# In the expert stage, weight splits and last products of the word conversion move from GpSimd to VectorE, sign and magnitude to ScalarE

## The chip, the cores and the metric

The kernel runs on one core of a Trainium2 chip. The metric is the device time of one execution in microseconds (us); the median of several executions is compared. TensorE (PE) multiplies, with weight loads (PEld) beside it; VectorE (DVE), ScalarE (ACT) and GpSimd (POOL) work element by element; SyncE (SP) issues most DMAs. Each engine works through its own instructions in order.

## The reference

Three parts follow each other: an attention whose scores below a threshold are dropped, a mixture of eight experts of which each token takes one, and a dense layer with the activation h - tanh(h). Weights of the dense layer (`w_in`, `w_out`) are float64.

```python
scores = scale * q @ k.T; thresh = max(scores) - tau
attn = exp(where(scores >= thresh, scores, -1e9) - max); attn /= sum(attn)
x = attn @ v                                   # 2304 tokens x 512

expert_idx = argmax(x @ w_gate)                # one of E = 8 experts for each token
h = maximum(xe @ w1[e], 0.0)                   # w1[e]: 512 x 1024
out[mask] = gate_w * (h @ w2[e])               # w2[e]: 1024 x 512

h = x @ w_in                                   # 512 x 2048, float64 weights
return ((h - tanh(h)) @ w_out).astype(float32) # 2048 x 512
```

## The kernel before

The three parts run after each other: attention to about 350 us, routing to about 370, the experts to about 650, the dense layer to the end. In the experts and the dense layer each matrix product is made three times on TensorE, from high and low parts of the operands: high is the value rounded to a short mantissa (a ScalarE copy to fp32r), low is the rest (a subtraction).

**Groups.** The expert stage is a row of 72 groups of work, numbered g: nine passes (the experts ranked by token count, the second one in two passes) of 256, 256, 288, 416, 384, 336, 320, 288 and 272 tokens, and eight groups for each pass. In group g, `h_exp` makes 12 matmuls into one of two PSUM buffers; `relu` (L1075, L1076) takes the high part by ScalarE and the low one by VectorE into `hbuf`; then come the jobs that the planner has put into group g; then `y_exp` makes the 12 matmuls of the second product for group g - 2. So `h` of group g + 2 waits until VectorE has read `h` of group g.

**The jobs** are entered by `plan` through `at(group, function)`, and in one group they are issued in the order in which `plan` enters them: token gathers (GpSimd, `gather_exp`, an indirect DMA, ten groups ahead of their pass), transposes of the gathered tokens (TensorE, one PSUM buffer "t"), their evacuation into high and low parts (L1027 by ScalarE, L1031 by VectorE), weight loads (`wload`, SP, four or five groups ahead) and weight splits (`wsplit`), loads of the dense layer, the late part of the routing (from group 8 on, a job in every second group), and last the word conversion.

**Weight splits.** `wload` brings 128 x 1024 words of w1 or w2 into one of four `raw` buffers. `wsplit` copies the high part by ScalarE (L1008) and subtracts it (L1010): by VectorE for w1, by GpSimd for w2 (all j = 1 with r < E). For the dense layer (r == E) the table `"eng"` says which engine subtracts.

**The word conversion.** `conv` turns the float64 words of the dense layer's weights into float32, 128 x 512 values at a time, in 32 conversions that start at the groups of the table `"conv"` (0 to 57). Its four steps stand in the groups start + 0, 3, 4 and 5 (table `"cv"`): `load` (SP, into one of three `cv` buffers); `bits` (three VectorE instructions: shift of the high word, L1155, joining with the low word, L1157, a mask for very negative values, L1159); `sign` (magnitude by ScalarE, L1163, a sign of -1, 0 or 1 by VectorE, L1164, their product by GpSimd, L1166); `store` (SP, to DRAM). The buffer `cm` has two halves that conversions use in turn, so that conversion n + 2 writes its half only after conversion n is stored.

Of the kernel before, what the change touches and what calls it, by code (L numbers as in the profile page):

```python
# [11 lines left out]
F32 = mybir.dt.float32  # L12
F32R = mybir.dt.float32r
F16 = mybir.dt.float16
BF16 = mybir.dt.bfloat16
I32 = mybir.dt.int32
U32 = mybir.dt.uint32
AF = mybir.ActivationFunctionType
ALU = mybir.AluOpType
# [409 lines left out]
E, F1, F2 = 8, 1024, 2048  # L429
# [466 lines left out]
LY = 2  # L896
# [22 lines left out]
class Mlp(Moe):  # L919
# [86 lines left out]
    def wsplit(self, r, i, j):  # L1006
        h, l, raw = self.W.pop((r, i, j, "raw"))
        self.nc.scalar.copy(h, raw)  # L1008
        pool = j if r < E else self.TB["eng"][2 * i + j] == "P"
        (self.nc.gpsimd if pool else self.nc.vector).tensor_tensor(out=l, in0=raw, in1=h.bitcast(F32), op=ALU.subtract)  # L1010


# [125 lines left out]
    def conv(self, i, h):  # L1138
        nc = self.nc
        T = 3.4332275390625e-05  # L1140
        st = {}

        def load():
            t = self.sp.tile([128, 1024], F32R, tag="cv", name="cv", bufs=3).bitcast(U32)
            nc.sync.dma_start(out=t.rearrange("p (a b) -> p a b", a=2) if i < 8 else t, in_=self.src64[i][h])
            r = t.rearrange("p (n t) -> p n t", t=2)
            st["lo"], st["hi"] = r[:, :, 0], r[:, :, 1]
            st["hf"] = st["hi"].bitcast(F32)
            if self.cm is None:
                self.cm = self.sp.tile([128, 1024], F32R, tag="cm", name="cm")  # L1150
            st["m"] = self.cm.bitcast(F32)[:, 512 * h:512 * h + 512]

        def bits():
            m = st["m"].bitcast(U32)
            nc.vector.tensor_scalar(out=m, in0=st["hi"], scalar1=3, scalar2=0x40000000,  # L1155
                                    op0=ALU.logical_shift_left, op1=ALU.bitwise_xor)
            nc.vector.scalar_tensor_tensor(out=st["lo"], in0=st["lo"], scalar=29, in1=m,  # L1157
                                           op0=ALU.logical_shift_right, op1=ALU.bitwise_or)
            nc.vector.tensor_scalar(out=st["m"], in0=st["hf"], scalar1=-T, scalar2=None, op0=ALU.is_le)  # L1159

        def sign():
            c = st["lo"].bitcast(F32)
            nc.scalar.activation(out=c, in_=c, func=AF.Abs)  # L1163
            nc.vector.scalar_tensor_tensor(out=st["m"], in0=st["hf"], scalar=T, in1=st["m"],  # L1164
                                           op0=ALU.is_ge, op1=ALU.subtract)
            nc.gpsimd.tensor_tensor(out=st["m"], in0=st["lo"].bitcast(F32), in1=st["m"], op=ALU.mult)  # L1166

        def store():
            nc.sync.dma_start(out=self.wscr[i, :, 512 * h:512 * h + 512], in_=st["m"])

        return [load, bits, sign, store]


    def x_load(self, k):
# [83 lines left out]
    def early2(self):  # L1258

        for i, j in FIRST:  # L1260
# [5 lines left out]
          "last": ((-3, -2), (-1, 1), (-2, 0), (0, 2), (-1, 2), (0, 3), (1, 2), (4, 6), (-60, -55), (-53, -50), (-7,  # L1266
                  -1), (-6, -4), (5, 10), (9, 11), (11, 12), (12, 14)), "x0": (12, 9, 7), "x": (14, 13, 8),
          "conv": (0, 1, 3, 5, 7, 10, 11, 13, 15, 16, 18, 20, 21, 23, 25, 28, 29, 32, 33, 35, 37, 38, 40, 42, 44, 46,
                  47, 51, 52, 54, 57, 57), "cv": (0, 3, 4, 5), "eng": "DPDPDPDPDPPDDDPP"}

    def plan(self, K):
        at = self.at
# [86 lines left out]
```

## Time and profile before

| | us |
|---|---|
| median of 3 runs (1075.16 to 1082.88) | 1077.63 |
| the profiled execution | 1076.63 |
| its span in the profile | 1074.5 |
| busy: TensorE / VectorE / GpSimd / ScalarE | 957.3 / 895.3 / 730.7 / 671.5 |

A busy time is the sum of an engine's instructions. It contains time in which an instruction has started and is held up by another engine, so one instruction's duration can be several times that of its fastest twin. The granted clock is TensorE's, 1.00 being the full one.

### The profile page before, as it was taken

To read this page: it belongs to the slowest core of one execution; us is meant where nothing else is said; L and a number is where in the kernel's file an instruction comes from. 1 tells how busy PE (TensorE), PEld (TensorE's weight loads), DVE (VectorE), ACT (ScalarE), POOL (GpSimd) and SP (SyncE) were. 2 spreads that over 40 slices of the span, in tenths; PEclk is the share of its full clock that TensorE was granted. 3 is DMA by queue.
4 is the path that set the end of the run, shared out by engine and by line. 5 is a ranking of instruction groups with operands and counts; after the bars stand their busy time and mean duration, and the time that the engine had idled before them with its cause. 6 is when DMAs were issued, how large, how long until landed. Compare 5 with 4: busy or idle time off the path is not lost.

```text
span 1074.5 us, 20770 instructions
## 1 busy us (share of the span) xinstructions
PE 957.3 (89%) x7342; PEld 876.6 (82%) x7342; DVE 895.3 (83%) x1635; ACT 671.5 (62%) x1262; POOL 730.7 (68%) x645
## 2 busy tenths in 40 slices
PE   4688897887787488999999988999999999999997
PEld 3576786776677387989999988888999999998986
DVE  5899888888884698977798876998989889888894
ACT  5797887986974154444455557666665666656662
POOL 3897887886874364455656567787867768677763
PEclk9698888898988599999999999999999999999999
DMA  6798999998989485877787976220101101000000
GB/s 160 145 213 165 211 205 152 225 202 163 175 155 169 149 292 199 278 227 247 258 290 252 295 247 177 76 76 20 40 8 38 30 20 40 8 31 1 20 11 30
DMA packets 247368, 153.16 MB, mean 143 GB/s; under 512 B 179642, under 2 KB 222028, under 8 KB 247261
## 3 DMA queue, kind: packets, MB, share of 16 engines
q1 hardware_dynamic: 243501, 141.02, 53.2%
q0 software_dynamic: 3312, 10.49, 2.8%
q8 instruction: 59, 0.97, 0.4%
q14 instruction: 48, 0.39, 0.1%
q10 hardware_dynamic: 448, 0.30, 0.1%
HBM read 85.08 MB, written 23.60 MB: 101 GB/s over the span
## 4 chain that ended last, share of the span: by engine, by line
PE 50%; DVE 9%; issue 3%; DMA 2%; ACT 1%; POOL 0%; another core or an unknown queue 0%; POOLq 0%; DVEq 0%; SPq 0%; ACTq 0%
PE h L1040 25%; PE y L1123 15%; PE y L1095 9%; DVE w L1236 2%; DVE w L1237 2%; PE t L1017 1%; DVE w L1234 1%; DMA xr<-rows,idx 1%; DVE cv L1157 1%; DVE tm L1235 1%; DVE w L1238 1%; DMA raw<-in_moe_w_dram 1%; DVE w L1010 1%; DMA raw<-wscr 0%; DVE cm L1159 0%
## 5 line engine op out<-in xcount | busy, mean ns | idle before, releaser
L265 POOL TENSOR_TENSOR e<-em,e 128x1024 f16<-128x1024 f32 (+1 forms) x98 | 158.1, 1613 | 55.0 <-ACT e L261 23.5
L1233 POOL TENSOR_SCALAR tm<-u 128x384 uint8<-128x384 f32 x88 | 129.7, 1474 | 51.4 <-ACT u L1229 50.8
L1040 PE MATMUL h<-xa,w 128*128 128x256 f32 (+6 forms) x864 | 140.5, 313 | 7.6 <-DVE hbuf L1076 6.8
L1095 PE MATMUL y<-hbuf,w 128*128 128x256 f32 (+6 forms) x864 | 139.5, 310 | 0.6 <-ACT yo L1098 0.6
L1040 PEld LDWEIGHTS h<-xa,w 128*128 128x128 f32 x864 | 130.5, 194 | 9.9 <-DVE hbuf L1076 8.1
L240 ACT ACTIVATE e<-sps,n 128x576 f32<-128x576 f32 x144 | 110.6, 768 | 34.8 <-DVE n L234 33.7
L1010 POOL TENSOR_TENSOR w<-raw,w 128x1024 fp32r<-128x1024 f32 x36 | 91.8, 2551 | 56.0 <-ACT w L1008 28.8
L1095 PEld LDWEIGHTS y<-hbuf,w 128*128 128x128 f32 x864 | 127.5, 191 | 1.3 <-ACT yo L1098 0.8
L1236 DVE SCALAR_TENSOR_TENSOR w<-y,w 128x384 f32<-128x384 f32 x96 | 123.3, 1284 | 0.0
L1229 ACT ACTIVATE u<-h 128x384 f32<-128x384 f32 x96 | 47.1, 491 | 117.3 <-PE h L1040 116.4
L253 DVE SCALAR_TENSOR_TENSOR em<-sps,n,e 128x576 f32<-128x576 f32 x144 | 116.6, 810 | 4.0 <-ACT e L240 2.4
L234 DVE TENSOR_REDUCE n<-sps 128x1 f32<-128x576 f32 x144 | 107.1, 744 | 12.3 <-PE sps L226 11.8
L1250 POOL TENSOR_TENSOR gl<-w,gh 128x384 fp32r<-128x384 f32 x83 | 85.7, 1032 | 38.0 <-ACT gh L1249 38.0
L1040 PE MATMUL h<-xk,w 128*128 128x384 f32 x576 | 109.6, 338 | 0.7 <-DVE w L1010 0.5
L297 PE MATMUL ops<-vh,et 128*128 128x64 f16 (+1 forms) x2240 | 97.4, 201 | 13.0 <-DVE x L303 12.1
L1040 PEld LDWEIGHTS h<-xk,w 128*128 128x128 f32 x576 | 102.1, 188 | 5.6 <-DVE w L1010 1.3
L297 PEld LDWEIGHTS <-et 128*128 128x128 f16 (+1 forms) x2240 | 83.6, 107 | 25.3 <-issue 21.1
L261 ACT CAST e<-em 128x576 f16<-128x576 f32 x144 | 99.9, 695 | 1.2 <-DVE em L253 1.2
L1075 ACT ACTIVATE hbuf<-h 128x256 fp32r<-128x256 f32 (+6 forms) x72 | 31.2, 433 | 108.3 <-PE h L1040 108.2
L226 PE MATMUL sps<-ka,qa 128*128 128x288 f32 x320 | 87.7, 367 | 9.4 <-DVE em L253 5.7
L1008 ACT CAST w<-raw 128x1024 fp32r<-128x1024 f32 x72 | 75.6, 1051 | 21.4 <-DVE free L597 11.6
L1123 PE MATMUL y<-w,gh 128*128 128x512 f32 x258 | 81.1, 395 | 3.2 <-POOL w L1010 1.5
(228 smaller groups left out, 2296.8 us busy)
## 6 DMA issues: line engine op xcount, KB each, us to landing
raw<-in_moe_w_dram SPq DMA_DIRECT2D x64, 512.0 KB, 5.2
cv<-in_moe_w_in_dram SPq DMA_DIRECT2D x16, 512.0 KB, 5.0
cv<-in_moe_w_out_dram SPq DMA_DIRECT2D x16, 512.0 KB, 5.4
wscr<-cm SPq DMA_DIRECT2D x32, 256.0 KB, 3.2
raw<-wscr SPq DMA_DIRECT2D x16, 512.0 KB, 3.8
xw<-yT SPq DMA_DIRECT2D x24, 192.0 KB, 2.7
vv<-in_v_dram SPq DMA_DIRECT2D x8, 512.0 KB, 5.1
raw<-in_q_dram SPq DMA_DIRECT2D x6, 576.0 KB, 7.7
```

Source lines behind the costliest of these rows:

```text
L234: nc.vector.tensor_reduce(out=n[:, 0:1], in_=ps[:, :, 0:288], axis=AX.XY, op=ALU.max, negate=True)
L240: nc.scalar.activation(out=e, in_=ps[:, :, 0:288], func=AF.Exp, bias=n[:, 0:1])
L253: nc.vector.scalar_tensor_tensor(out=self.em[u, g][:, i].rearrange("p (a b) -> p a b", a=2), in0=ps[:, :, 0:288], scalar=n[:, 1:2], in1=e, ...
L261: self.nc.scalar.copy(self.e16[u, g][:, i, 0:S], self.em[u, g][:, i])
L265: eng.tensor_tensor(out=e16[:, r, S + 64:], in0=em[:, r, 0:512], in1=e16[:, r, 0:512], op=ALU.subtract)
L297: nc.tensor.matmul(o[q], lhsT=et[:, base + c, q], rhs=vh[:, a, j, c if c < 5 else c - 5, :], start=(n == 0), stop=(n == len(terms) - 1))
L1010: (self.nc.gpsimd if pool else self.nc.vector).tensor_tensor(out=l, in0=raw, in1=h.bitcast(F32), op=ALU.subtract)
L1040: self.nc.tensor.matmul(out, lhsT=a, rhs=b, start=(i == 0), stop=(i == len(parts) - 1))
L1095: nc.tensor.matmul(self.ys[d], lhsT=a[:, f % 2, s], rhs=b, start=(f == 0 and i == 0), stop=(f == 7 and i == 2))
L1123: nc.tensor.matmul(self.ys[m], lhsT=a[:, s], rhs=b[:, f % 2], start=(f == 0 and i == 0), stop=(f == 15 and i == 2))
L1233: nc.gpsimd.tensor_scalar(out=mk, in0=u, scalar1=RCUT * RCUT, scalar2=None, op0=ALU.is_gt)
L1236: V.scalar_tensor_tensor(out=w, in0=y, scalar=b, in1=w, op0=ALU.add, op1=ALU.mult)
```

## The change

In the expert stage GpSimd keeps only the gathers (and the dense layer's splits that its table gives it). VectorE subtracts for w2 too. In the conversion a new step `mag` takes the sign by ScalarE into a bf16 tile `sg` and makes the high word's magnitude in place, also by ScalarE; `bits` clamps this magnitude from below at T by VectorE, in place of the mask, and shifts the clamped word; `sign` is left with ScalarE's magnitude of the joined word; a new step `mul` makes the product by VectorE. The six steps stand at start + 0, 2, 3, 4, 5 and 5: `mul` and `store` are in the same group.

```diff
@@ def wsplit(self, r, i, j):
-        pool = j if r < E else self.TB["eng"][2 * i + j] == "P"
+        pool = r == E and self.TB["eng"][2 * i + j] == "P"
         (self.nc.gpsimd if pool else self.nc.vector).tensor_tensor(out=l, in0=raw, in1=h.bitcast(F32), op=ALU.subtract)
@@ def conv(self, i, h):
+        def mag():
+            st["sg"] = self.sp.tile([128, 512], BF16, tag="gh", name="sg", bufs=LY + 1)
+            nc.scalar.activation(out=st["sg"], in_=st["hf"], func=AF.Sign)
+            nc.scalar.activation(out=st["hf"], in_=st["hf"], func=AF.Abs)
+
         def bits():
             m = st["m"].bitcast(U32)
-            nc.vector.tensor_scalar(out=m, in0=st["hi"], scalar1=3, scalar2=0x40000000,
+            nc.vector.tensor_scalar(out=st["m"], in0=st["hf"], scalar1=T, scalar2=None, op0=ALU.max)
+            nc.vector.tensor_scalar(out=m, in0=m, scalar1=3, scalar2=0x40000000,
                                     op0=ALU.logical_shift_left, op1=ALU.bitwise_xor)
             nc.vector.scalar_tensor_tensor(out=st["lo"], in0=st["lo"], scalar=29, in1=m,
                                            op0=ALU.logical_shift_right, op1=ALU.bitwise_or)
-            nc.vector.tensor_scalar(out=st["m"], in0=st["hf"], scalar1=-T, scalar2=None, op0=ALU.is_le)
 
         def sign():
             c = st["lo"].bitcast(F32)
             nc.scalar.activation(out=c, in_=c, func=AF.Abs)
-            nc.vector.scalar_tensor_tensor(out=st["m"], in0=st["hf"], scalar=T, in1=st["m"],
-                                           op0=ALU.is_ge, op1=ALU.subtract)
-            nc.gpsimd.tensor_tensor(out=st["m"], in0=st["lo"].bitcast(F32), in1=st["m"], op=ALU.mult)
+
+        def mul():
+            nc.vector.tensor_tensor(out=st["m"], in0=st["lo"].bitcast(F32), in1=st["sg"], op=ALU.mult)
 
-        return [load, bits, sign, store]
+        return [load, mag, bits, sign, mul, store]
@@ TB
-                  47, 51, 52, 54, 57, 57), "cv": (0, 3, 4, 5), "eng": "DPDPDPDPDPPDDDPP"}
+                  47, 51, 52, 54, 57, 57), "cv": (0, 2, 3, 4, 5, 5), "eng": "DPDPDPDPDPPDDDPP"}
```

## Rows read from the trace of the kernel before

**Rows 1.** Stretches: us; length, PE, PEld, DVE, ACT, POOL busy (x); clock, DMA, GB/s
```profile
392.60:428.60 36.00, 29.29 (x228) 28.56 (x229) 31.99 (x51) 15.53 (x31) 20.66 (x12) 0.95 0.65 227
457.00:470.00 13.00, 10.47 (x72) 9.80 (x71) 12.57 (x18) 4.42 (x8) 7.25 (x6) 0.87 0.74 237
470.00:600.00 130.00, 130.00 (x822) 128.53 (x821) 105.89 (x140) 65.03 (x118) 76.22 (x44) 1.00 0.80 263
600.00:640.00 40.00, 36.67 (x277) 35.96 (x277) 29.25 (x40) 22.11 (x43) 23.42 (x12) 1.00 0.82 261
640.00:680.00 40.00, 35.97 (x215) 32.08 (x215) 30.68 (x37) 26.70 (x48) 30.63 (x18) 1.00 0.60 179
```

**Rows 2.** Timeline from 389 to 393 us: start, length, instruction [idle before <-releaser]
```profile
389.06 2.84 POOL L1010 TENSOR_TENSOR w<-raw,w 128x1024 fp32r<-128x1024 f32 x1
389.69 2.50 DVE L1159 TENSOR_SCALAR cm<-cv 128x512 f32<-128x512 f32 x1
392.57 1.70 PE L1040 MATMUL h<-xa,w 128*128 128x256 f32 x12 [1.47 <-DVE hbuf L1076]
```

**Rows 3.** Timeline from 394 to 411 us
```profile
394.70 1.79 POOL L1057 DMA_INDIRECT xr<-rows,idx  x1
396.01 0.69 DVE L1157 SCALAR_TENSOR_TENSOR cv<-cv,cm 128x512 uint32<-128x512 uint32 x1
...
401.65 0.63 PE L1017 MATMUL t<-ident,xr 128*128 128x128 f32 x4 [1.62 <-DMA xr<-rows,idx]
...
408.77 0.74 DVE L1031 TENSOR_TENSOR xa<-t,xa 128x384 fp32r<-128x384 f32 x2
...
409.62 1.09 PE L1017 MATMUL t<-ident,xr 128*128 128x128 f32 x4 [4.46 <-issue]
```

**Rows 4.** Timeline from 460 to 468 us, PE and DVE
```profile
460.10 2.77 DVE L1159 TENSOR_SCALAR cm<-cv 128x512 f32<-128x512 f32 x1
...
463.42 4.09 PE L1040 MATMUL h<-xa,w 128*128 128x416 f32 x12 [2.53 <-DVE hbuf L1076]
```

**Rows 5.** Timeline from 616 to 634 us
```profile
616.39 2.78 DVE L1157 SCALAR_TENSOR_TENSOR cv<-cv,cm 128x512 uint32<-128x512 uint32 x1
...
621.57 1.85 PE L1040 MATMUL h<-xa,w 128*128 128x288 f32 x12 [2.17 <-DVE hbuf L1076]
...
633.78 1.40 PE L1095 MATMUL y<-hbuf,w 128*128 128x272 f32 x9 [0.62 <-ACT yo L1098]
```

**Rows 6.** Conversion: instructions xcount, ns min/median/max; the store's DMA; who waited for it
```profile
L1157 DVE SCALAR_TENSOR_TENSOR cv<-cv,cm x32: 692/696/2867, 382.3 to 620.0; 128x512 uint32<-128x512 uint32 x32
L1159 DVE TENSOR_SCALAR cm<-cv x32: 426/428/2819, 383.0 to 620.7; 128x512 f32<-128x512 f32 x32
L1163 ACT ACTIVATE cv<-cv x32: 669/686/705, 385.2 to 620.8; 128x512 f32<-128x512 f32 x32
L1164 DVE SCALAR_TENSOR_TENSOR cm<-cv,cm x32: 675/683/3558, 386.9 to 622.0; 128x512 f32<-128x512 f32 x32
...
  DVE cm L1155: 0.3, 1
...
DMA to landing us min/median/max: 2.0/3.2/4.7
```

**Rows 7.** Weight split L1010 on both engines, whole span, ns min/median/max
```profile
L1010 DVE TENSOR_TENSOR w<-raw,w x36: 1200/1226/2267, 362.2 to 669.9; 128x1024 fp32r<-128x1024 f32 x36
L1010 POOL TENSOR_TENSOR w<-raw,w x36: 2349/2432/2926, 365.4 to 685.8; 128x1024 fp32r<-128x1024 f32 x36
```

**Rows 8.** DVE groups by form, 392.6 to 428.6 us: xcount | busy us, mean ns
```profile
L1010 DVE TENSOR_TENSOR w<-raw,w 128x1024 fp32r<-128x1024 f32 x4 | 7.6, 1908 | 0.7 <-ACT w L1008 0.7
L1164 DVE SCALAR_TENSOR_TENSOR cm<-cv,cm 128x512 f32<-128x512 f32 x5 | 6.3, 1256 | 0.0
L1076 DVE SCALAR_TENSOR_TENSOR hbuf<-h,hbuf 128x256 fp32r<-128x256 f32 x9 | 3.7, 416 | 1.9 <-ACT hbuf L1075 1.8
```

**Rows 9.** ScalarE's table loads in the whole span: xcount | busy us, mean ns
```profile
L51 ACT ACT_TABLE_LOAD x1 | 1.3, 1283 | 0.8 <-PEq L1344 0.8
```

## The prediction

> **What bounds the kernel now.** I read the page's busy slices first, then the busy time by stretch, then the timeline wherever TensorE is not full. From 470 to 600 us TensorE is busy for all of 130.0 us at clock 1.00: nothing on the other engines can make that stretch shorter. What the change can win lies where TensorE waits [rows 1, 2]: 1.47 us at 391, 6.71 between 392.6 and 428.6, 2.53 between 457 and 470, 3.33 between 600 and 640, and 4.03 between 640 and 680, where the dense layer already runs.
>
> The timeline then shows what is late. At 389.69 VectorE's mask, 428 ns at its median [rows 6], takes 2.50 us beside a GpSimd w2 split, and ends only after that split has; the `hbuf` instruction behind it is late, and TensorE waits 1.47 us [rows 2]. The same picture stands at 460 (2.77 us, TensorE waits 2.53) [rows 4] and at 616 (a join of 696 ns takes 2.78; TensorE waits 2.17) [rows 5, 6]. Around 400 there are two causes. A gather starts late, at 394.70, and TensorE waits 1.62 us for its tokens; then VectorE reaches the evacuation L1031 only at 408.77, and the next transposes, which need that PSUM buffer, wait 4.46 us [rows 3]. So VectorE, held by GpSimd, is the bound in the passes of 256 and 288 tokens, and TensorE elsewhere.
>
> **GpSimd loses** 32 w2 splits of 2.43 us, 78 us of work [rows 7], and 32 products. None of it is on TensorE's path by itself; what counts is VectorE's waiting and the gathers, which stand behind it in GpSimd's queue.
>
> **VectorE, the conversion.** Removed: mask 0.428 and sign 0.683. Added: a clamp, of the mask's form and input, at 0.428, and a product of two SBUF inputs over 512 elements, nearest to the sign instruction, at 0.683 (bounds: 0.428 by the mask's row, 1.226 by the split of twice the size). Difference 0 by my values, within -0.3 and +0.5 us for each of 32 [rows 6, 7]. The shift now reads a packed tile instead of every second word; I leave its price as it is.
>
> **VectorE, the splits.** 32 splits at 1.226 us are 39 us more work [rows 7]. Whether it fits is decided by stretch. In 392.6 to 428.6 VectorE is busy 31.99 of 36.0 us [rows 1]. Four splits at 1908 ns instead of 1226 and five signs at 1256 instead of 683 hold 5.6 us of being held up [rows 8], which goes; four w2 splits of the second expert (its i = 0 to 3) fall into the same groups and bring 4.9. That gives 31.3 us. TensorE needs 29.3 busy, 1.0 to 1.8 of it lost to the clock, so about 28. VectorE is then slightly over TensorE's need, not under it. It may run behind, because `h` of group g + 2 waits only for the `hbuf` of group g. Going by hand through groups 7 to 15 in program order, VectorE falls up to a group behind, and one evacuation is late by about 1.3 us. In 470 to 600, even with nothing given back, 105.9 + 16 x 1.226 = 125.5 of 130.0 us: it fits.
>
> A rule bears on this. The Trainium skill, GPSIMD Engine Reference, sections Specifications and Key points, says that GpSimd shares its SBUF interfaces with VectorE, with contention for VectorE instructions that run in a 2-port mode or have two SBUF inputs. The trace agrees: the `hbuf` instruction, which reads one input from PSUM, averages 416 ns in the worst stretch, while splits and signs, with two SBUF inputs, are stretched [rows 8]. It would make the moved splits safe only once GpSimd is quiet.
>
> What stays on GpSimd beside them are the gathers. One join ran at 0.69 us, its usual length, entirely inside a gather of 1.79 us [rows 3]: I count gathers as no hold.
>
> **ScalarE** gets 64 instructions of 128 x 512: Sign and magnitude at 0.686 each by L1163 [rows 6], 44 us in all, 1.37 for each conversion. From 392.6 to 428.6 it is busy 15.5 of 36.0 and gets four or five conversions, so about 22; from 470 to 600, 65 of 130 and 16 more conversions, so 87 [rows 1]. Cover is there. `mag` waits for the load in group + 2, one group earlier than anything waited for it; behind it on ScalarE stands the next group's `relu`. A wait of up to a group costs nothing, since `y` follows two groups later; I take 0, at most 1 us for each of the ten conversions of the short groups.
>
> **SP and the new wait.** `store` stands with `mul` in one group, and the first VectorE instruction of conversion n + 2 writes the same half of `cm`. Twelve of the 30 pairs start three groups apart, so that this clamp is one group behind the `mul`. The store lands 3.2 us after its issue [rows 6]; a short group is 2.9 to 3.2 us of matmuls (two lots of twelve at 1.70 us, less their overlap [rows 2]). Before, the product could run in the group earlier; VectorE waited for a store once, 0.3 us [rows 6]. Now it waits in up to four pairs in the short groups, 0.6 to 1.9 us each: 0 to 7.6 us, of which TensorE's slack takes a part. I take 2.5. In the longer groups landing is covered. Behind the held clamp stand joins, `hbuf` and evacuations; SP itself holds the next conversion's load behind the store, as it did behind GpSimd's product.
>
> **The sum.** Regained at most: 1.47 + 6.71 + 2.53 + 3.33 = 14.0 us of waiting, and clock: 0.95 over 36.0 and 0.87 over 13.0 us are 1.8 + 1.7 at most [rows 1]; at 463.42 twelve matmuls of 416 columns took 4.09 [rows 4]. I take 2.7, together 16.7. Given back: the late evacuation 1.3, the stores 2.5, about 1.0 at 460 (a dense-layer split stays on GpSimd, and a w2 split joins VectorE's queue), 0.6 at 633, where TensorE waits for a ScalarE copy [rows 5]. Net 16.7 - 5.4 = 11.3. The 4.03 us at 640 to 680 stay: those splits keep their engine by the table. From the profiled 1076.63 that is 1065.3. The median lies 1.0 above the profiled run, inside the runs' spread; I leave the sum as it is.
>
> **Rivals.**
>
> *All comes back.* VectorE's lag stays under a group and stores land in time: 14.0 + 2.7, and up to 2 us of the 640 to 680 stretch through earlier free `raw` buffers: 1058 to 1060. For it: the largest wait, 4.46, needs only two unheld instructions. Against: 31.3 of about 28 us.
>
> *VectorE is the bound by itself.* The short groups run at VectorE's pace with every wait for ScalarE and the stores added, 35 us as now, and only the waits at 391, 460 and 616 go: about 4 us, 1072.5. For it: the same 31.3 us. Against: the queue may run behind.
>
> *The store's wait replaces the held instructions, and the kernel is slower.* Place: the clamp behind the `mul` in the twelve pairs. Price: 3.2 us landing less 0.42 of `hbuf`, up to 2.8 us each, 33 in all. It decides when the average wait of the twelve passes 16.7/12 = 1.4 us on TensorE's path; slower by over 1% needs 2.3. At full price 1093. Against: groups of 320 to 416 columns outlast the landing.
>
> *Sign is not in the loaded table.* The trace shows one table load, 1.283 us [rows 9], though Exp, Tanh, Square, Abs and copies all run; if Sign needed another, each conversion would load twice, 32 x 2 x 1.283 = 82 us on ScalarE, and in 470 to 600 it would hold 87 + 41 of 130 us, so be the bound there with every wait: about 1090. The Trainium skill, ScalarE: Activation LUTs, section Table sets, names relu, copy, identity and abs as filler of every set and does not name Sign there; by its 2.66 us with the drain it would be 170 us of ScalarE. No run here shows Sign. Against: Sign is as simple as the functions that share the loaded set.
>
> **How the numbers follow.** Net forecast (1060 to 1070) 0.45; all comes back 0.20; VectorE the bound 0.27; stores slower 0.05; table 0.03. One per cent of the time, 10.8 us, is about what a measurement can tell from none: faster means under 1066.9. Of the forecast about two thirds lie there (0.30), with all of the first rival: 0.50. Slower are the last two: 0.08. The rest, 0.42, is within 1%. The range leaves out the slower rivals and the tips: 1057 to 1076.
>
> **What would show it.** In the changed profile the mask's successor and the join keep 0.43 and 0.70 us as means, not only medians; L1010 on VectorE averages under 1.3; TensorE's waits at 391, 400 to 410, 460 and 619 are gone; clock 1.00 from 380 on. Wrong would be: VectorE busy over 95% and TensorE under 90% in the passes of 256 and 288 tokens; many waits of the clamp for `wscr`; more than one table load; ScalarE's `relu` waiting behind `mag`; or stretched VectorE instructions beside gathers.

## The result, and the profile after

The changed kernel takes 1066.27 us in the median (1065.0 to 1070.1), the kernel before 1076.49 beside it; the ratio is 0.9899, 95% interval 0.9852 to 0.9947. A second set beside other runs of the kernel before gave 0.9895 (0.9871 to 0.992). So the gain is 1.0 to 1.1%, right at the one per cent that the prediction took for the edge of what can be told. The profiled execution took 1065.0 us, its span 1063.3.

First the busy time by stretch, for the stretches of [rows 1] (us; length, PE, PEld, DVE, ACT, POOL busy; clock, DMA, GB/s):

```profile
392.60:428.60 36.00, 33.63 (x265) 33.07 (x264) 29.46 (x61) 23.44 (x44) 3.14 (x3) 0.95 0.76 258
457.00:470.00 13.00, 12.90 (x77) 12.66 (x78) 10.53 (x21) 8.20 (x20) 2.65 (x3) 1.00 0.87 292
470.00:600.00 130.00, 130.00 (x837) 128.67 (x836) 97.31 (x161) 86.89 (x155) 9.20 (x10) 1.00 0.81 263
600.00:640.00 40.00, 38.63 (x295) 37.92 (x295) 28.54 (x40) 24.21 (x40) 6.85 (x4) 1.00 0.85 277
640.00:680.00 40.00, 35.92 (x188) 31.71 (x187) 34.34 (x42) 27.04 (x51) 31.03 (x19) 1.00 0.42 127
```

TensorE's gap (length less busy) went from 6.71 to 2.37 us in the first of them, from 2.53 to 0.10 in the second, from 3.33 to 1.37 in the fourth; with the 1.47 us at 391, which are gone, that is 10.2 us regained. The stretches are fixed in time and the work has moved forward in them, so a wait can fall across an edge; over the whole expert stage, from its first to its last product, the gap fell from 14.5 to 4.9 us, by 9.6. The last stretch kept its gap: 4.03 before, 4.08 now. The clock of the second rose from 0.87 to 1.00, that of the first stayed at 0.95.

Next the instructions of the conversion (count: ns min/median/max, first and last start), and what VectorE waited for at the clamp from 360 to 690 us (busy, mean ns, then idle before it by releaser). They answer to [rows 6]:

```profile
L1160 DVE TENSOR_SCALAR cm<-cv x32: 418/422/551, 385.3 to 610.6; 128x512 f32<-128x512 f32 x32
L1161 DVE TENSOR_SCALAR cm<-cm x32: 426/428/431, 385.8 to 611.1; 128x512 uint32<-128x512 uint32 x32
L1163 DVE SCALAR_TENSOR_TENSOR cv<-cv,cm x32: 692/694/749, 386.3 to 611.5; 128x512 uint32<-128x512 uint32 x32
L1171 DVE TENSOR_TENSOR cm<-cv,sg x32: 672/685/687, 391.5 to 616.0; 128x512 f32<-128x512 f32 x32
...
L1160 DVE TENSOR_SCALAR cm<-cv 128x512 f32<-128x512 f32 x32 | 13.6, 426 | 3.0 <-issue 1.3 <-DVE cm L1171 0.9 <-DMA wscr<-cm 0.8
```

The maxima of 2.8 to 3.6 us are gone. No conversion instruction is longer than 0.75 us, though 26 gathers of 0.86 to 1.88 us still run on GpSimd. Besides them and one dense-layer split, GpSimd makes four other two-input instructions in the expert stage (L1203, at its end); two of VectorE's instructions L1196, 0.53 us by themselves, took 1.37 us beside those.

What is left around 400 us is in the timeline (start, length, instruction, idle before), and it answers to [rows 3]:

```profile
402.29 0.68 DVE L1171 TENSOR_TENSOR cm<-cv,sg 128x512 f32<-128x512 f32 x1
402.89 0.42 DVE L1160 TENSOR_SCALAR cm<-cv 128x512 f32<-128x512 f32 x1
...
403.34 0.43 DVE L1161 TENSOR_SCALAR cm<-cm 128x512 uint32<-128x512 uint32 x1
...
403.80 0.69 DVE L1163 SCALAR_TENSOR_TENSOR cv<-cv,cm 128x512 uint32<-128x512 uint32 x1
404.41 0.42 DVE L1076 SCALAR_TENSOR_TENSOR hbuf<-h,hbuf 128x256 fp32r<-128x256 f32 x1
...
404.75 0.75 DVE L1031 TENSOR_TENSOR xa<-t,xa 128x384 fp32r<-128x384 f32 x2
...
405.59 0.63 PE L1017 MATMUL t<-ident,xr 128*128 128x128 f32 x4 [2.19 <-issue]
```

Nothing is held up here. VectorE simply has the new product, the three conversion instructions and `hbuf` in its queue ahead of the evacuation L1031, and the transposes, which need the PSUM buffer that L1031 empties, wait 2.19 us. Before, it was 4.46.

### The profile page after: what moved, and what is told of

Same layout as the page of the kernel before. It is cut to its first block, busy times and chain, and to the rows that moved or that the text cites. A ratio compares the mean times of both kernels' runs of the same rounds, so it can differ in the third digit from the quotient of the medians.

```text
span 1063.3 us, 20657 instructions
## 1 busy us (share of the span) xinstructions
PE 954.2 (90%) x7342; PEld 875.2 (82%) x7342; DVE 872.7 (82%) x1667; ACT 711.3 (67%) x1326; POOL 602.1 (57%) x581
## 4 chain that ended last, share of the span: by engine, by line
PE 52%; DVE 20%; ACT 11%; DMA 7%; issue 6%; SPq 2%; POOL 1%; another core or an unknown queue 0%; POOLq 0%; DVEq 0%; ACTq 0%
PE h L1040 22%; PE y L1123 15%; PE y L1095 8%; ACT e L240 4%; DVE em L253 3%; DMA raw<-in_moe_w_dram 3%; ACT e L261 2%; PE sps L226 2%; DVE w L1242 2%; DVE n L234 2%; DVE w L1241 2%; DVE qb L209 2%; PE ops L297 2%; DMA vv<-in_v_dram 1%; PE tps L167 1%
## 5 line engine op out<-in xcount | busy, mean ns | idle before, releaser
L1241 DVE SCALAR_TENSOR_TENSOR w<-y,w 128x384 f32<-128x384 f32 x96 | 121.2, 1262 | 0.0
L1057 POOL DMA_INDIRECT xr<-rows,idx x26 | 27.2, 1046 | 162.6 <-PE t L1017 157.6
L1010 DVE TENSOR_TENSOR w<-raw,w 128x1024 fp32r<-128x1024 f32 x68 | 83.5, 1231 | 19.9 <-ACT w L1008 19.2
L1242 DVE SCALAR_TENSOR_TENSOR w<-y,w 128x384 f32<-128x384 f32 x96 | 79.6, 829 | 10.0
## 6 DMA issues: line engine op xcount, KB each, us to landing
cv<-in_moe_w_in_dram SPq DMA_DIRECT2D x16, 512.0 KB, 10.2
```

Source lines behind the costliest of these rows:

```text
L1241: V.scalar_tensor_tensor(out=w, in0=y, scalar=b, in1=w, op0=ALU.add, op1=ALU.mult)
```

## The experiments

All figures of the table come from the profiled execution of each kernel, by one row of the view by stretch from the start of the first to the start of the last product `h<-xa` of the experts. "Gap" is its length less TensorE's busy time. "Held" is, summed over VectorE's conversion and weight-split instructions, the duration above what they take undisturbed (0.42, 0.43, 0.69, 0.68 and 1.22 us); other instructions that were held are not in it. "Rest" is the span's end less that last product, the dense layer. The ratio and median are from the timed runs.

| kernel | median us | ratio to before, interval | experts | gap | VectorE busy | held | rest |
|---|---|---|---|---|---|---|---|
| before | 1076.49 | | 278.5 | 14.5 | 227.3 | 57.3 | 426.0 |
| after | 1066.27 | 0.9899 (0.9852 to 0.9947) | 267.2 | 4.9 | 204.4 | 0 | 424.6 |
| e1_splits | 1067.53 | 0.9879 (0.986 to 0.9898) | 268.1 | 6.5 | 221.3 | 18.8 | 425.6 |
| e2_conv | 1078.00 | 0.9988 (0.9967 to 1.0009) | 281.2 | 14.9 | 202.3 | 34.1 | 424.9 |
| e3_hold2 | 1085.96 | 1.0048 (1.003 to 1.0067) | 290.9 | 22.8 | 238.5 | 35.8 | 425.5 |
| e4_alldve | 1066.04 | 0.9856 (0.9824 to 0.9888) | 269.5 | 7.5 | 203.2 | 0.2 | 423.0 |
| e5_thin | 1066.81 | 0.9871 (0.9833 to 0.9908) | 269.5 | 8.4 | 205.7 | 0.1 | 424.9 |
| e6_hold1 | 1073.93 | 0.9953 (0.993 to 0.9976) | 274.6 | 10.4 | 216.6 | 13.0 | 424.5 |
| e7_halves | 1078.46 | 0.9985 (0.9967 to 1.0003) | 278.4 | 14.8 | 220.3 | 49.9 | 425.6 |
| e8_thin_alldve | 1063.99 | 0.9848 (0.9798 to 0.9898) | 267.0 | 6.4 | 204.0 | 0.6 | 422.9 |
| e9_vload | 1077.07 | 0.9972 (0.9956 to 0.9988) | 278.7 | 12.2 | 233.2 | 2.8 | 424.8 |
| e10_splits_alldve | 1064.35 | 0.9852 (0.983 to 0.9874) | 267.8 | 6.6 | 220.0 | 17.6 | 422.7 |
| e11_after (after again) | 1069.50 | 0.9895 (0.9871 to 0.992) | 270.1 | 6.7 | 205.7 | 0.3 | 424.6 |
| e12_best (e8 again) | 1065.33 | 0.985 (0.9826 to 0.9875) | 268.5 | 6.3 | 203.2 | 0.5 | 423.3 |

The kernel before stood at 1079.34, 1078.96 and 1080.6 us beside e1 to e4, e5 to e8 and e9 to e12; medians of different sets differ by that much, so ratios are compared. One kernel's expert stage varies by up to 3 us (after and e11).

**e1_splits: only the w2 splits move.** The conversion stays as it was.

```diff
 # the kernel before, with
-        pool = j if r < E else self.TB["eng"][2 * i + j] == "P"
+        pool = r == E and self.TB["eng"][2 * i + j] == "P"
```

> Only the 32 w2 splits move to VectorE; the conversion stays as in the kernel before, with its product on GpSimd. Theory A (the gain is VectorE no longer held up by GpSimd's elementwise work): 78 of some 120 us of GpSimd's work go, so about two thirds of the 10 us: 1069 to 1072 us, VectorE's splits at 1.23 us mean except beside products, TensorE's waits at 391 and 460 gone. Theory B (the gain is gathers that start earlier): only the wait of 1.6 us at 400 goes: 1074 to 1076. Theory C (VectorE's extra 39 us cost what the holds gave): 1076 or more.

**e2_conv: only the conversion moves.** The changed kernel with the w2 splits back on GpSimd.

```diff
 # the changed kernel, with
-        pool = r == E and self.TB["eng"][2 * i + j] == "P"
+        pool = j if r < E else self.TB["eng"][2 * i + j] == "P"
```

> Only the conversion changes (sign and magnitude on ScalarE, product on VectorE); the w2 splits stay on GpSimd. Theory A: 32 holds by the product go, those by the splits stay, so about a third of the gain: 1072 to 1074 us, with masks and joins still at 2.5 us beside a split. Theory B: gathers still stand behind splits: 1075 to 1077. The two parts together should give the whole gain if they add up: the sum of the gains of this run and of the run with the splits alone is about 10 us.

The splits alone bring all of the gain (0.9879), the conversion alone nothing that can be told (0.9988), and the conversion on top of the splits nothing either. Both expectations missed: two thirds and one third of the gain were expected, 1069 to 1072 and 1072 to 1074 us, and 1067.53 and 1078.00 were measured. With the conversion alone the old picture stays, as the timeline of e2_conv shows:

```profile
405.56 0.69 DVE L1171 TENSOR_TENSOR cm<-cv,sg 128x512 f32<-128x512 f32 x1
405.86 2.58 POOL L1010 TENSOR_TENSOR w<-raw,w 128x1024 fp32r<-128x1024 f32 x1 [5.94 <-ACT w L1008]
406.16 2.57 DVE L1160 TENSOR_SCALAR cm<-cv 128x512 f32<-128x512 f32 x1
...
410.16 0.75 DVE L1031 TENSOR_TENSOR xa<-t,xa 128x384 fp32r<-128x384 f32 x2
...
411.01 1.09 PE L1017 MATMUL t<-ident,xr 128*128 128x128 f32 x4 [5.03 <-issue]
```

The clamp, 0.42 us by itself, stands until GpSimd's split is over, everything behind it is 2.15 us later than in the changed kernel, and TensorE waits 5.03 us instead of 2.19. e2 also shows that VectorE's total is no measure: it is busy 202.3 us there and 204.4 in the changed kernel, and the gap is 14.9 against 4.9.

**e3_hold2: two-input work goes back to GpSimd.** The changed kernel with extra work whose result nobody reads: subtracts of 384, 384 and 128 elements on GpSimd behind each w2 split. The splits themselves are on VectorE and come out early.

```diff
 # wsplit of the changed kernel, at its end
+        if r < E and j:
...
+            for o, n in ((0, 384), (384, 384), (768, 128)):
+                self.nc.gpsimd.tensor_tensor(out=self.dm[:, 0:n], in0=self.dm[:, 0:n],
+                                             in1=h.bitcast(F32)[:, o:o + n], op=ALU.subtract)
```

> The changed kernel, and GpSimd subtracts something that nobody needs (three instructions, 896 elements per partition, two inputs, about 2.4 us in all) after ScalarE's copy for each w2 split, so VectorE has the work of the changed kernel and GpSimd the activity of the kernel before. Theory A: VectorE is held again, with all the splits in its queue: 1076 to 1090 us, VectorE's medians unchanged and its means up by half. Theory B: no VectorE instruction is longer and the gathers alone are later: 1067 to 1069. If only the amount of VectorE work mattered: 1066.

It becomes slower than the kernel before: 35.8 us held, a gap of 22.8. It is not the kernel before again: less is held there than the 57.3 us of that kernel, but VectorE has the 32 splits in its queue as well. The clamp's median and maximum rise from 422 and 551 ns in the changed kernel to 584 and 1656, and TensorE's waits from 372 to 665 us (us in total, times, longest) say by which way the time is lost:

```profile
L1166 DVE TENSOR_SCALAR cm<-cv x32: 411/584/1656, 387.1 to 633.3; 128x512 f32<-128x512 f32 x32
...
PE t L1023 <- issue: 10.1, 4, 4.6
PE h L1046 <- DVE hbuf L1082: 6.2, 3, 3.3
...
PE t L1023 <- DMA xr<-rows,idx: 1.7, 1, 1.7
```

16.3 us are evacuations and `hbuf` that VectorE delivers late; one wait of 1.7 is for gathered tokens, though the gathers stand behind the extra work in GpSimd's queue. So it is mostly VectorE's waiting, not the gathers' lateness, that costs.

**e6_hold1: the same, with one input.** Multiplications by 1.0 in place of the subtracts, extra work as well.

```diff
 # wsplit of the changed kernel, at its end
+        if r < E and j:
...
+            for o, n in ((0, 384), (384, 384), (768, 128)):
+                self.nc.gpsimd.tensor_scalar(out=self.dm[:, 0:n], in0=h.bitcast(F32)[:, o:o + n],
+                                             scalar1=1.0, scalar2=None, op0=ALU.mult)
```

> As the run with GpSimd's unneeded subtraction, but the unneeded instructions multiply one input by a constant (one read, same three pieces per w2 split). If what holds VectorE is GpSimd's access to memory by any elementwise instruction: VectorE's means rise as there and the time is 1080 to 1088. If only two-input GpSimd instructions hold it: VectorE's means stay at their medians and the time is 1066 to 1070.

GpSimd is about as busy as in e3 (155.6 us against 146.9 in the experts), but VectorE is held 13.0 us instead of 35.8. The timeline of e6_hold1 shows how little each instruction is stretched, and that it still adds up ahead of the evacuation:

```profile
407.62 3.22 POOL L1015 TENSOR_SCALAR dm<-w 128x384 f32<-128x384 f32 x3 [0.67 <-ACT w L1008]
407.82 0.73 DVE L1165 TENSOR_SCALAR cm<-cv 128x512 f32<-128x512 f32 x1
408.58 0.63 DVE L1166 TENSOR_SCALAR cm<-cm 128x512 uint32<-128x512 uint32 x1
409.25 0.87 DVE L1168 SCALAR_TENSOR_TENSOR cv<-cv,cm 128x512 uint32<-128x512 uint32 x1
...
411.21 0.63 PE L1022 MATMUL t<-ident,xr 128*128 128x128 f32 x4 [3.57 <-issue]
```

The three are 0.69 us longer than undisturbed, and the wait is 3.57 us in place of the 2.19 of the changed kernel. The 1073.93 us lie between the two expectations (1066 to 1070, 1080 to 1088): one-input work on GpSimd costs VectorE time too, but about a third of it.

**e7_halves: GpSimd's split in two.** The kernel before, each w2 split of the experts made by GpSimd in two instructions of 512 elements.

```diff
 # wsplit of the kernel before
-        (self.nc.gpsimd if pool else self.nc.vector).tensor_tensor(out=l, in0=raw, in1=h.bitcast(F32), op=ALU.subtract)
+        for o in ((0, 512) if j and r < E else (0,)):
+            c = slice(o, o + (512 if j and r < E else 1024))
+            (self.nc.gpsimd if pool else self.nc.vector).tensor_tensor(out=l[:, c], in0=raw[:, c], in1=h.bitcast(F32)[:, c], op=ALU.subtract)
```

> The kernel before with each w2 split on GpSimd made in two instructions of 512 elements, of the product's size. The runs with one part each say that the splits' holds cost 10 us and the products' next to nothing. Theory L (what counts is the length of one hold: 2.4 us is more than TensorE's slack, 1.3 us is not; VectorE gets in between the halves): 1067 to 1073. Theory T (two halves behind each other hold as long as one whole, or the total counts): 1076 to 1080, and VectorE instructions of 2.5 us and more remain.

No difference (0.9985), and the total held is little smaller (49.9 against 57.3 us). The timeline of e7_halves shows the two ways in which it comes about (its POOL lines join both halves):

```profile
406.91 2.67 DVE L570 TENSOR_TENSOR keep<-keep 128x18 int32<-128x18 f32 x1
407.01 2.52 POOL L1012 TENSOR_TENSOR w<-raw,w 128x512 fp32r<-128x512 f32 x2
...
412.48 0.87 PE L1019 MATMUL t<-ident,xr 128*128 128x128 f32 x3 [4.44 <-issue]
...
543.47 2.89 POOL L1012 TENSOR_TENSOR w<-raw,w 128x512 fp32r<-128x512 f32 x2 [2.59 <-issue]
543.70 1.52 DVE L1157 TENSOR_SCALAR cm<-cv 128x512 uint32<-128x512 uint32 x1
545.25 1.66 DVE L1159 SCALAR_TENSOR_TENSOR cv<-cv,cm 128x512 uint32<-128x512 uint32 x1
```

At 406.91 an instruction over 18 elements per partition, which takes 0.18 us by itself, begins just before the first half, takes 2.67 and ends 0.05 us after the second half. That is the rarer case: in the trace, 4 of the 31 pairs of halves in the expert stage hold one instruction through both. In 16 pairs VectorE gets in between: an instruction that began under the first half ends after that half, before the second has ended, as the shift at 543.70 does (1.52 us instead of 0.42). The next one may then be held by the second half, as the join behind it is (1.66 instead of 0.69).

**e9_vload: the same time, without a hold.** The changed kernel with extra work on VectorE: two subtracts of 384 elements behind each w2 split.

```diff
 # wsplit of the changed kernel, at its end
+        if r < E and j:
...
+            for o, n in ((0, 384), (384, 384)):
+                self.nc.vector.tensor_tensor(out=self.dm[:, 0:n], in0=self.dm[:, 0:n],
+                                             in1=h.bitcast(F32)[:, o:o + n], op=ALU.subtract)
```

> The changed kernel with two unneeded VectorE subtracts of 384 elements behind every w2 split of the experts (32 splits; extra work whose result nobody reads). By the 386-element subtract of the trace (some 0.42 to 0.7 us each) that is 0.8 to 1.4 us a split, 27 to 45 us of VectorE in all, spread as the holds of the splits were in the kernel before (38 us in all), but without any hold by GpSimd. Theory 'the time of VectorE in the short passes is what costs': TensorE waits again and the kernel takes 1070 to 1078 us, near the kernel before. Theory 'VectorE has slack, and what cost was that the split itself came out late (2.4 us on GpSimd)': 1065 to 1069 us.

VectorE's groups and TensorE's waits of e9_vload:

```profile
L1016 DVE TENSOR_TENSOR dm<-dm,w 128x384 f32<-128x384 f32 x60 | 34.1, 568 | 1.0
...
PE t L1023 <- issue: 4.7, 2, 2.9
PE h L1046 <- DVE w L1010: 2.3, 4, 0.9
PE h L1046 <- DVE hbuf L1082: 2.3, 3, 1.3
```

34.1 us of plain work behind the w2 splits cost about what e2 loses: the experts take 278.7 us, against 281.2 there and 267.2 to 270.1 in the changed kernel. (That e2 has 34.1 us of holds is chance; its splits come out later too.) No hold and no late split is needed for the loss; VectorE's time ahead of evacuations, `hbuf` and later splits is enough.

**e5_thin: the queue at 403 us thinned.** The changed kernel with the 32 conversions spread more evenly over the groups; **e4_alldve**: the changed kernel with all splits of the dense layer on VectorE too; **e8_thin_alldve**: both.

```diff
 # e5_thin and e8_thin_alldve: the table of the changed kernel, the entry "conv" alone
-          "conv": (0, 1, 3, 5, 7, 10, 11, 13, 15, 16, 18, 20, 21, 23, 25, 28, 29, 32, 33, 35, 37, 38, 40, 42, 44, 46,
-                  47, 51, 52, 54, 57, 57)
+          "conv": (0, 1, 3, 6, 9, 12, 14, 17, 19, 20, 22, 24, 25, 27, 29, 30, 32, 34, 35, 37, 39, 40, 42, 44, 45, 47,
+                  49, 50, 52, 54, 55, 57)
 # e4_alldve, e8_thin_alldve and e10_splits_alldve: the entry "eng" alone
-          "eng": "DPDPDPDPDPPDDDPP"
+          "eng": "DDDDDDDDDDDDDDDD"
```

> The changed kernel with the starts of the 32 conversions spread: one conversion fewer before group 7, two groups apart in the short passes, closer in the long ones. If VectorE's queue in groups 7 to 15 is what leaves the wait of 2.2 us at 403 and the clock's dip behind it, both go and the time falls by 2 to 4 us to 1062 to 1064. If those waits come from somewhere else, no change: 1066.

> The changed kernel with the eight dense-layer splits that the table gives to GpSimd made by VectorE too. Theory A: each takes 1.23 us of VectorE instead of holding it for about 2.7, so the 4 us that TensorE waits between 640 and 680 shrink by 1 to 3: 1063 to 1065 us. Rival (VectorE is full in the dense layer, 95% busy, so its own work counts): 8 x 1.23 us are added: 1068 to 1076.

> The spread conversions and all dense-layer splits on VectorE together. If the two add up: 1060 to 1064. If the dense layer's gain was noise: as the run with the spread alone.

In e5 the wait at 405 us shrinks from 2.19 to 0.32, but others of 0.8 to 1.7 us come at 418, 422, 457 and 460, and the gap is no smaller (8.4). Neither e5 (1066.81 us; 1062 to 1064 or no change expected) nor e4 (1066.04; 1063 to 1065 expected) can be told from the changed kernel by the intervals of the table. With every split on VectorE the dense layer takes 422.7 to 423.3 us in the four profiles that have it (e4, e8, e10, e12) and 424.5 to 425.6 in the others but the kernel before, which has 426.0. That is a gain of 1 to 2 us; in the experts such a kernel shows none. The rival of e4's expectation had VectorE 95% busy in the dense layer; it is busy for 361.0 of 410 us there (changed kernel, 650 to 1060 us), 88%.

**e10_splits_alldve, e11_after, e12_best**, together on one chip. The first is e1 with all dense-layer splits on VectorE; the others are the changed kernel and e8_thin_alldve once more.

> The kernel before with all splits of weights on VectorE, those of the dense layer too, and the word conversion left as it was. If the conversion's move is needed for nothing and the dense layer gains its 2 us as in the two runs with all splits on VectorE: 1063 to 1066 us. If the products still on GpSimd cost something beside the splits: 1067 to 1070 us.

> The changed kernel once more, beside the others on one chip, to know what the differences of 1 to 3 us among the variants are worth: ratio 0.986 to 0.993 expected, 1064 to 1070 us.

> The variant of the conversions spread evenly with all splits on VectorE once more, in five rounds. If the dense layer's 2 us are real it stands 1 to 3 us under the changed kernel of the same call: ratio 0.983 to 0.987, 1062 to 1065 us. If they are noise it stands level with it.

e10 leaves the conversion as it was before the change and stands at 0.9852, 1064.35 us (1062.55 to 1065.22), the changed kernel beside it at 0.9895, 1069.50 us (1067.42 to 1071.38): with the old conversion, and every split on VectorE, the kernel is faster than the one before and the changed one. The kernel that differs from e10 in the conversion alone is e4, and its ratio, from another set, is the same, 0.9856: the conversion's move is worth nothing that shows. Of the 6.5 us between the spans of e10 and e11 the dense layer has 1.9; the rest is 2.3 us in the experts, within what one kernel varies, and 2.3 us before them, where the two do the same. The stretch that was the worst, and the timeline of e10_splits_alldve around 400 us:

```profile
392.60:428.60 36.00, 33.46 (x272) 32.54 (x271) 35.00 (x63) 17.50 (x37) 16.63 (x12) 1.00 0.74 265
...
392.86 1.32 POOL L1166 TENSOR_TENSOR cm<-cv,cm 128x512 f32<-128x512 f32 x1 [3.21 <-ACT w L1008]
394.33 1.79 POOL L1057 DMA_INDIRECT xr<-rows,idx  x1
...
398.99 1.30 POOL L1166 TENSOR_TENSOR cm<-cv,cm 128x512 f32<-128x512 f32 x1 [1.38 <-ACT w L1008]
399.11 2.27 DVE L1010 TENSOR_TENSOR w<-raw,w 128x1024 fp32r<-128x1024 f32 x1
...
401.13 0.63 PE L1017 MATMUL t<-ident,xr 128*128 128x128 f32 x4 [1.48 <-DMA xr<-rows,idx]
...
404.30 0.74 DVE L1031 TENSOR_TENSOR xa<-t,xa 128x384 fp32r<-128x384 f32 x2
...
405.14 0.63 PE L1017 MATMUL t<-ident,xr 128*128 128x128 f32 x4 [0.51 <-PE h L1040]
```

VectorE is busy for 35.00 of 36.0 us, and TensorE does more there (272 matmuls against 265) than beside the changed kernel's 29.46; its gap is 2.54 us, against 2.37 there. GpSimd's product at 398.99 stretches a split by 1.05 us. The tokens that TensorE waits for at 401.13, 1.48 us, come from the gather at 394.33, which stands behind the product at 392.86 in GpSimd's queue; in the changed kernel the last gather before 400 us started at 380.22. In the changed kernel the product stands in VectorE's queue ahead of the evacuation, and TensorE waits 2.19. At this place the two are a trade.

## Why the prediction was right, and where its steps were not

**The net.** 11.3 us were forecast for the span's 1074.5; it fell by 11.2, and so did the expert stage, by 11.3. The median of 1066.27 is 1.0 above the forecast 1065.3. So close a match is luck: profiled again (e11), the changed kernel's expert stage is 270.1 us, 2.9 longer. The mechanism, VectorE held by GpSimd's two-input instructions, is shown: e3 brings it back, with VectorE's splits kept, and loses more than the change had won, and e6 loses less with one-input work of about the same length.

**What came back.** 10.2 of the 14.0 us of waiting; forecast were 14.0 less 5.4, and 2.7 of clock. The clock rose where it was at 0.87 and not where it was at 0.95, so that its term was too large by about one us: behind the wait of 2.19 us that is left at 405.59, the granted clock is 0.50 from 408 to 410 us, 1.2 instead of 2.4 GHz.

**What was given back** was forecast at 5.4 us, and 4.6 us of waits are found by place. The two are near each other by errors that cancel:

- the late evacuation, 1.3 forecast: 2.19, and the clock beside it;
- the stores, 2.5 forecast: VectorE was idle 3.0 us at the clamp, of which 0.8 for stores, and no wait of TensorE came of it;
- 460 us, 1.0 forecast: 0.54, at 457.10; 633 us, 0.6 forecast: none;
- not forecast: 1.13 us at 608, where a w1 split waits for ScalarE's copy of a load that arrived late, and 0.7 in three small waits at 379, 407 and 613.

**VectorE's demand** of 31.3 us against 28 was the step that was wrong in size, and it carried 0.27 of the chances. It took 5.6 us of holds out of the stretch, from two groups of [rows 8], splits and signs. Two smaller groups of the same view, small routing instructions, were left out (kernel before, then after, 392.6 to 428.6 us):

```profile
L727 DVE CAST keep<-keep 128x18 bf16<-128x18 f32 x3 | 2.8, 919 | 0.1
L570 DVE TENSOR_TENSOR keep<-keep 128x18 int32<-128x18 f32 x1 | 2.5, 2520 | 0.0
```

```profile
L1010 DVE TENSOR_TENSOR w<-raw,w 128x1024 fp32r<-128x1024 f32 x8 | 9.8, 1223 | 2.0 <-ACT w L1008 2.0
L727 DVE CAST keep<-keep 128x18 bf16<-128x18 f32 x3 | 0.5, 178 | 0.1
L570 DVE TENSOR_TENSOR keep<-keep 128x18 int32<-128x18 f32 x1 | 0.2, 179 | 0.0
```

They were held 3 x 0.74 + 2.34 = 4.6 us. With them the demand would have come out at 26.7, under TensorE's 28, and VectorE as the bound by itself would have had little for it. Measured are 29.46 us busy, with one more conversion and more groups in the stretch than before. That not everything came back in spite of it points to the order in the queue, not the total: e10 shows a VectorE at 35.00 of 36 us and TensorE waiting no longer than 2.54 us in the stretch.

**The conversion on VectorE** at no cost: clamp, shift, join and product take 0.42, 0.43, 0.69 and 0.68 us, as priced. But the prediction counted the holds by GpSimd's product as part of what is to be won, and e2 and e1 show that this part is worth nothing measurable. VectorE's own conversion work is the same in e1 and in the changed kernel (mask and sign go, clamp and product come), so the 18.8 us of holds that e1 has more cost nothing that shows. Why they cost so little beside e9's 34.1 us is only argued: those of e10's timeline are of about one us, at a split that TensorE isn't waiting for. It isn't settled whether the length of one hold or its place decides.

**ScalarE**: 22 and 87 us forecast, 23.44 and 86.89 measured. Its Sign needed no other table; the view of ScalarE's groups still has one load, as in [rows 9]:

```profile
L51 ACT ACT_TABLE_LOAD x1 | 1.3, 1283 | 0.8 <-PEq L1349 0.8
```

**Gathers** hold nothing that counts: the longest of 128 conversion instructions is 0.75 us, and of the 17 that ran during a gather none took more than 0.13 us above its shortest twin. The row that the prediction took it from was misread: the join ended at 396.70, the gather at 396.49 [rows 3], so that it did not lie entirely inside.

**The rivals** fall: not all came back (3.8 us of waits stay in the three stretches before 640, and the clock of the first); VectorE isn't the bound by its total; the stores' wait was 0.8 us, not 33; there was one table load. The 640 to 680 us stretch stayed as forecast, and e4 and e10 show what it holds: 1 to 2 us in the dense layer, once its splits leave GpSimd as well.

## What to carry to other kernels

Where VectorE's instructions have maxima of several times their median, look on GpSimd for a two-input instruction that ends with them, and sum the holds over all groups, the smallest instructions too. Moving that instruction to VectorE can pay even though VectorE gets more work: with the w2 splits added, its busy time in the experts fell from 227.3 to 221.3 us (e1). Then undo the parts of the change one at a time: here one line of it held the gain, and the larger rest could be left out.

## What the runs showed of the hardware

In the expert stage of the kernel before, 46 of VectorE's instructions on SBUF tiles began under a two-input GpSimd instruction, and all 46 ended after it, by 0.03 to 1.09 us. The hold does not depend on how much VectorE's instruction has to do: 18 elements per partition took 2.67 us instead of 0.18 (e7), and a clamp, with one input, 2.57 instead of 0.42 (e2). Halving GpSimd's instruction changes little in the sum (49.9 us held against 57.3) and nothing in the time (0.9985). GpSimd with one input stretched the clamp to 0.73 us at most, and 8 of the 13 clamps that began under such an instruction ended before it (e6). The Trainium skill, SBUF — State Buffer, section SBUF: two separate sides, says that the port pair that VectorE and GpSimd share is an exclusive lock held for the whole instruction, and that the other one blocks fully; it says so of VectorE instructions in a 2-port mode or with two SBUF inputs. The two-input runs agree with it; the one-input run doesn't show a full block. VectorE's `hbuf`, with one input in PSUM, wasn't held by either: its 256-token form took at most 0.43 us in every run.
